# Attention backward, dP rows: laid out by key quarters and turned by VectorE straight from PSUM, with the products issued later

## The chip, the cores and the metric

The kernel runs on one core of a Trainium2 chip. Its figure is the device time of one execution in microseconds (us); less is better. Times are those of whole executions; the profile is of one execution, whose span is a little shorter than its time.

## The reference

One decode step (one new token for each of 4 sequences) through a transformer block, and the gradients of everything by one vector `grad_out`:

```python
x = A_x                                            # 4 x 1 x 512
h  = x + attn(layernorm(x), k_cache, v_cache, wq, wo)   # 32 heads, 4096 keys, head size 128
h2 = h + silu_mlp(layernorm(h), w1, w3, w2)             # inner size 1792
out, vjp = jax.vjp(f, x, k_cache, v_cache, wq, wo, w1, w3, w2)
return (out, *vjp(grad_out))
```

For one (batch, head) pair with query q, keys K, values V (4096 x 128 each, bf16), probabilities P and output gradient dO, the backward pass needs

- dV = P times dO (an outer product, 4096 x 128),
- dP = V dO (one number for each key), c = dO . O (one number),
- dS = P (dP - c) / sqrt(128), and dK = dS times q (an outer product, 4096 x 128).

There are 128 such pairs ("heads" from here on). K and V are read (1 MB each), V a second time for dP, and dK and dV are written, 1 MB each.

## The kernel before, in words

**Storage.** Nearly everything large lives in `arena`, 23 slots of one head's 1 MB each (4160 bf16 in each of 128 partitions). Class `Slot` takes the slot at the head of the list `free`; giving it back appends it to the list. A slot's next writer waits for whatever last used it: a write that must land, or the engine that read it last. `Slot2` takes two neighbouring slots.

**Queues.** The schedule is written out by hand: each engine carries out its instructions in the order in which the program issues them. All large transfers are issued on SP's queue, in program order; a transfer that waits holds up those behind it. At most eight are under way at once, since each one waits for the one eight places earlier.

**Forward** (0 to about 660 us in the profile). K and V are streamed through for scores, softmax, and for M, a matrix from which dq comes later.

**Middle** (to about 700 us). MLP forward and backward, layernorms, and the first dO. Nine V loads for the second pass are issued on the way.

**Backward, single heads** (heads 0 to 31, `SP` = 32). Per head s:

- `load_V2` (L840) loads V into a slot. `vring` holds slots kept for further V loads.
- `front(s)`: four times `words_T` (L798, L799): TensorE turns four 128x128 blocks of V, as 32-bit words of two bf16, into PSUM, and ScalarE copies them back over V. Then eight matmuls (L1245) put dP rows of the head into one PSUM tile `dP_ps` that four heads share, and the V slot is given back. The stationary operands come from `zd`, which `dO_window` (L1211, GpSimd) fills two heads ahead.
- every four heads `rows_out` (L1221) copies that tile to SBUF on ScalarE and `rows_T` (L1228) turns it by four TensorE transposes into PSUM tile `dPT_ps`, both from inside the next head's `front`; `group_dS` (L1261, L1264) makes dS of four heads on VectorE.
- `grad_V` and `grad_K` take a slot, make the outer product on VectorE (L813) and issue its write (L824, L1271).

`front` runs five heads ahead of `grad_K` (`L` = 5), and `grad_V` runs nine or fewer ahead of it through `more_V`. Before the loop, five fronts are issued with

```python
            front(s)
            if s == 0:
                for gv in first_gv:
                    gv.give()
            more_V((4, 6, 7, 8, 9)[s])
```

so that the gradients of heads 2 and 3 follow `front(0)`, of 4 and 5 `front(1)`, and of 6, 7 and 8 one front each. `first_gv` holds the two slots of `grad_V(0)` and `grad_V(1)`, which were issued in the middle part. `side` spreads the work on wo, dq and the weight gradients over the heads.

**Backward, pairs** (heads 32 to 127 as 48 pairs t). The same with two heads in one 2 MB transfer, each on 64 partitions: `front_pair` (L1328 for the products, three pairs ahead), `group_dS_pair` (L1342, L1345; four instructions on 64 partitions each for two pairs), `grad_pair` (L1400 on VectorE, write L1410), `dO_pair` (L1308, GpSimd) for the stationary operands.

Of the kernel before, what the change touches and what calls it, by code (L numbers as in the profile page):

```python
# [21 lines left out]
SP = 32  # L22
# [5 lines left out]
def kernel(  # L28
# [769 lines left out]
            nc.tensor.transpose(ptw[:, jj, :], w[:, 4 * g + jj, :], ident_f[:])  # L798
        nc.scalar.copy(out=v.rearrange("p (j d) -> p j d", d=Dh)[:, g * GW:(g + 1) * GW, :], in_=pt[:])  # L799

    def words_of(v, g, k):
        return v.rearrange("p (x r t) -> p t x r", r=Dh, t=2)[:, k, 4 * g:4 * g + 4]

    def V_T(s, ps, part=range(SJ // GW)):
        if s not in VTs:
# [26 lines left out]
    NV2 = 7  # L832
# [138 lines left out]

    with ExitStack() as c2:
        psT = c2.enter_context(tc.tile_pool(name="psT2", bufs=2, space=bass.MemoryType.PSUM))
        psD = c2.enter_context(tc.tile_pool(name="psD", bufs=1, space=bass.MemoryType.PSUM))
        psrep = c2.enter_context(tc.tile_pool(name="psrep", bufs=1, space=bass.MemoryType.PSUM))
        psg = c2.enter_context(tc.tile_pool(name="psg", bufs=2, space=bass.MemoryType.PSUM))
        psx = c2.enter_context(tc.tile_pool(name="psx", bufs=1, space=bass.MemoryType.PSUM))
# [215 lines left out]
        dS2s = {}  # L1193
        zd = [bw3.tile([P, 2, 32], BF16, name=f"zd{i}", tag=f"zd{i}", bufs=1) for i in range(B)]
        dOw = bw3.tile([P, 2, SP], BF16, name="dOw", tag="dOw", bufs=1)
        for i in range(B):
            nc.gpsimd.memset(zd[i][:], 0.0)

# [16 lines left out]
                P2s[s] = bw3.tile([P, SJ, 2], BF16, tag="P2", name="P2")  # L1215
                nc.gpsimd.tensor_copy(out=P2s[s][:], in_=P_all[:, s, :, None].to_broadcast([P, SJ, 2]))

        def rows_out():
            if "ps" in rows:
                rows["sb"] = bw3.tile([P, 512], FP32, tag="dPr", name="dPr", bufs=1)  # L1220
                nc.scalar.copy(out=rows["sb"][:], in_=rows.pop("ps")[:])  # L1221

        def rows_T():
            if "sb" in rows:
                sb = rows["t"] = rows.pop("sb")
                rows["T"] = psD.tile([P, B, P], FP32, tag="dPT", name="dPT_ps")
                for jj in range(4):
                    nc.tensor.transpose(rows["T"][:, jj, :], sb[:, jj * P:(jj + 1) * P], ident_f[:])  # L1228

        def front(s):  # L1230
            hl = s % B
            if s not in VTs:
                for g in range(SJ // GW):
                    V_T(s, psT, range(g, g + 1))
                    if hl == 0 and g == 0:
                        rows_out()
                    if hl == 0 and g == 2:
                        rows_T()
            v = VTs[s].t[:, 0:SJ * Dh]
            if hl == 0:  # L1240
                rows["acc"] = psD.tile([P, 512], FP32, tag="dP", name="dP_ps")
            dO_window(s + 2)
            for k in range(2):
                for c in range(4):
                    nc.tensor.matmul(rows["acc"][32 * c:32 * (c + 1), :], lhsT=zd[hl][:, k, :], rhs=words_of(v, c, k),  # L1245
                                     start=(hl == 0 and k == 0), stop=(hl == B - 1 and k == 1), tile_position=(0, 32 * c))
            if hl == B - 1:
                rows["ps"] = rows.pop("acc")
            sl = VTs.pop(s)
            if nv["next"] < SP and len(V2s) + len(VTs) + len(vring) < NV2:  # L1250
                vring.append(sl.i)
            else:
                gave(sl.i, stored=False)

        def group_dS(g):
            i0 = g * B
            T = rows.pop("T").rearrange("p jj (c m) -> p c jj m", c=4)
            t = rows.pop("t")[:, 0:B * SJ].rearrange("p (b j) -> p b j", b=B)
            t5 = t.rearrange("p b (c jj i) -> p b c jj i", c=4, i=2)
            for hl in range(B):  # L1260
                nc.vector.tensor_scalar(out=t5[:, hl], in0=T[:, :, :, 2 * hl:2 * hl + 2], scalar1=c_rep[:, i0 + hl:i0 + hl + 1],  # L1261
                                        scalar2=scale, op0=ALU.subtract, op1=ALU.mult)
# [21 lines left out]
        def two(t):  # L1284
            s = SP + t // B * 2 * B + t % B
            return s, s + B
# [16 lines left out]
        def dO_pair(t):  # L1303
            if t < NT:
                s, s2 = two(t)
                for i in range(2):
                    r_ = slice(64 * i, 64 * (i + 1))
                    nc.gpsimd.tensor_copy(out=zt[t % B][r_, :, ZP + 2 * i:ZP + 2 * i + 2], in_=zt[B][r_, :, s - SP:s2 - SP + 1:B])  # L1308

        def front_pair(t, mid):  # L1310
            pl = t % 2
            v = pV[t].t[:, 0:2 * SJ * Dh]
            for g in range(2 * SJ // GW):
                words_T(psT, v, g)
                if pl == 0 and g == 0:
                    rows_out()
                if pl == 0 and g == 2:
                    rows_T()
                if g == 3:
                    mid()  # L1320
            if pl == 0:
                rows["acc"] = psD.tile([P, 512], FP32, tag="dP", name="dP_ps")
            dO_pair(t + 2)
            for u in range(2):
                m = 16 * u + 4 * pl
                for k in range(2):
                    for c in range(4):
                        nc.tensor.matmul(rows["acc"][32 * c:32 * (c + 1), :], lhsT=zt[t % B][:, k, ZP - m:ZP - m + 32],  # L1328
                                         rhs=words_of(v, 2 * c + u, k), start=(pl == 0 and u == 0 and k == 0),
                                         stop=(pl == 1 and u == 1 and k == 1), tile_position=(0, 32 * c))  # L1330
            if pl == 1:
                rows["ps"] = rows.pop("acc")
            pV.pop(t).give()

        def group_dS_pair(g):
            T = rows.pop("T").rearrange("p jj (g z l i a) -> p z l a g jj i", g=8, z=2, l=2, i=2, a=2)
            t = rows.pop("t")[:, 0:4 * SJ].rearrange("p (l j) -> p l j", l=2)
            t6 = t.rearrange("p l (g jj i) -> p l g jj i", g=8, i=2)
            for l in range(2):
                for a, s in enumerate(two(2 * g + l)):  # L1340
                    r_ = slice(64 * a, 64 * (a + 1))
                    nc.vector.tensor_scalar(out=t6[r_, l], in0=T[r_, 0, l, a], scalar1=c_rep[r_, s:s + 1],  # L1342
                                            scalar2=scale, op0=ALU.subtract, op1=ALU.mult)
            pdS[g] = bw3.tile([P, 2, 2 * SJ, 2], BF16, tag="dS2", name="dS2", bufs=1)
            nc.vector.tensor_tensor(out=pdS[g][:], in0=t[:, :, :, None].to_broadcast([P, 2, 2 * SJ, 2]),  # L1345
                                    in1=P_two(2 * g)[:, :, :, None].to_broadcast([P, 2, 2 * SJ, 2]), op=ALU.mult)

        ZP = 20
        Pp, zt, P2b = {}, [], []

        def P_two(t, n=2):
# [2 lines left out]
        def P_rows(q):  # L1354
            if q >= NT // B or q in Pp:
                return
            if not Pp:
                Pp["s"] = Slot("Pp")
                x = Pp["s"].t[:, NT * 2 * SJ:]
                n = 2 * (ZP + 32)  # L1360
                zt.extend(x[:, n * i:n * (i + 1)].rearrange("p (k c) -> p k c", k=2) for i in range(B))
# [100 lines left out]
        for s in range(L):  # L1462
            load_ahead(s)
# [4 lines that stand above are left out]
            more_V((4, 6, 7, 8, 9)[s])  # L1468
            if s == 0:
                replicate("rdo", REP)  # L1470
        group_dS(0)
        for s in range(SP):
            part["B"] = s + 12 >= SP
# [8 lines left out]
            if s + L < SP:  # L1482
                front(s + L)
            elif (s + L - SP) % 2 == 0:
                if s + L == SP:
                    dO_words(zt[B], SP, NH)
                    dO_pair(0)
                    dO_pair(1)
                front_pair((s + L - SP) // 2, lambda: None)
# [3 lines left out]
            if s % B == B - 1:  # L1493
                if s + 1 < SP:
                    group_dS((s + 1) // B)
                else:
                    group_dS_pair(0)
            side(s)
        for t in range(NT):
            s = SP + 2 * t  # L1500
            load_pairs(t + LP)
# [2 lines left out]
            if t + LP < NT:  # L1504
                front_pair(t + LP, lambda: side(s))
            else:
                if t + LP == NT:
                    rows_out()
                    rows_T()
# [37 lines left out]
```

## Time and profile before

| | us |
|---|---|
| median of 3 executions | 1688.53 |
| lowest, highest | 1688.17, 1689.38 |
| profiled execution, its own time | 1688.41 |
| its span | 1686.6 |
| busy PE, DVE, ACT, POOL | 1260.6, 1233.9, 960.9, 379.6 |
| moved by DMA | 707.21 MB, mean 419 GB/s |

The mean granted TensorE clock was 0.855. PE is TensorE, DVE VectorE, ACT ScalarE, POOL GpSimd; SP issues the large transfers. "L813" is line 813 of the kernel. An entry such as `arena<-pt_tps` names what is written and what is read; `[0.93 <-DMA out_dram<-arena]` behind an instruction says that its engine was idle for 0.93 us before it, and that a transfer from the arena to an output ended the wait. In a table of stretches the columns are the stretch, its length, then the busy time and number of instructions of each engine, the granted clock, the DMA engines' mean busy share and what they moved.

### The profile page before, as it was taken

Reading aid. Unit: us, or ns where it says so; the run is one execution under the profiler, and the core shown is the slowest. Engines: PE = TensorE matmul, PEld = TensorE weight load, DVE = VectorE, ACT = ScalarE, POOL = GpSimd, SP = SyncE. Lnnn points to the kernel's source line nnn. Section 1 sums busy time; section 2 is a strip of 40 time slices with the busy share of each in tenths; the row PEclk is TensorE's granted clock in tenths of the full one; section 3 lists DMA queues with packets and bytes.
Section 4 is the critical chain, followed back from the end, with each engine's and each line's share of the span. In section 5 each row is a group of like instructions: output and inputs, shape, how many; then the busy total and the mean of one; then the engine's idle time right before and its main releaser. Section 6 shows DMA issues by size and latency. Waiting matters only on the chain.

```text
span 1686.6 us, 33967 instructions
## 1 busy us (share of the span) xinstructions
PE 1260.6 (75%) x14188; PEld 924.3 (55%) x14188; DVE 1233.9 (73%) x1198; ACT 960.9 (57%) x1492; POOL 379.6 (23%) x663
## 2 busy tenths in 40 slices
PE   5989888888888888878878666667766677776660
PEld 4777777677667766745555544544434444444440
DVE  5999899989998997667766476576565656555673
ACT  3455454445445454677666556666655676666650
POOL 1221222222232222234541131111120101011020
PEclk9999999999999999799899778777678676567775
DMA  9999999999999999999999999999999999999996
GB/s 400 424 424 424 425 423 425 424 424 421 418 423 411 424 411 397 398 410 426 425 426 428 429 429 429 431 430 429 429 430 430 429 429 431 430 429 431 430 429 259
DMA packets 80986, 707.21 MB, mean 419 GB/s; under 512 B 8748, under 2 KB 12984, under 8 KB 15296
## 3 DMA queue, kind: packets, MB, share of 16 engines
q1 hardware_dynamic: 80416, 704.94, 99.2%
q8 instruction: 112, 1.84, 0.4%
q14 instruction: 42, 0.34, 0.0%
q0 software_dynamic: 416, 0.10, 0.0%
HBM read 422.59 MB, written 282.34 MB: 418 GB/s over the span
## 4 chain that ended last, share of the span: by engine, by line
DMA 35%; DVE 7%; ACT 5%; PE 5%; issue 3%; DVEq 0%; SPq 0%; POOL 0%; ACTq 0%
DMA out_dram<-arena 34%; DVE arena L1400 7%; ACT arena L799 5%; PE pt_tps L798 1%; PE dq_ps L1007 1%; PE dP_ps L1245 1%; DMA arena<-in_A_v_cache_dram 1%; PE pt_wo L610 0%; DVEq L1542 0%; PE rep_ps L1186 0%; DVE dPr L1342 0%; ACT dPr L1221 0%; PE dOT_ps L773 0%; PE dPT_ps L1228 0%; PE c_ps L784 0%
## 5 line engine op out<-in xcount | busy, mean ns | idle before, releaser
L799 ACT COPY arena<-pt_tps 128x1024 bf16<-128x1024 bf16 x512 | 491.7, 1023 | 249.0 <-PE pt_tps L798 247.3
L798 PE MATMUL pt_tps<-ident_f,arena 128*128 128x128 f32 x2048 | 410.7, 356 | 202.9 <-DMA arena<-in_A_v_cache_dram 125.6
L798 PEld LDWEIGHTS pt_tps<-ident_f,arena 128*128 128x128 f32 x2048 | 304.1, 182 | 349.3 <-issue 191.6
L1400 DVE TENSOR_TENSOR arena<-arena 128x8192 bf16<-128x8192 bf16 x48 | 212.5, 4427 | 197.9 <-DMA out_dram<-arena 192.5
L457 DVE TENSOR_TENSOR arena<-arena 128x4096 bf16<-128x4096 bf16 x128 | 292.4, 2285 | 24.0 <-POOL arena L453 24.0
L472 PE MATMUL M_ps<-arena 128*128 128x130 bf16 x4096 | 286.9, 223 | 30.0 <-DMA arena<-in_A_v_cache_dram 29.2
L472 PEld LDWEIGHTS <-arena 128*128 128x128 bf16 x4096 | 254.6, 99 | 49.6 <-DMA arena<-in_A_v_cache_dram 42.5
L1400 DVE TENSOR_TENSOR arena<-dS,arena 128x8192 bf16<-128x8192 bf16 x48 | 212.3, 4424 | 67.6 <-DMA out_dram<-arena 67.6
L364 DVE STREAM_TRANSPOSE arena<-arena 128x512 f32<-128x512 f32 (+1 forms) x321 | 250.6, 797 | 0.0
L359 ACT COPY arena<-pt_tps 128x1024 bf16<-128x1024 bf16 x128 | 129.4, 1012 | 180.4 <-PE pt_tps L358 149.6
L1397 POOL COPY arena<-arena 128x128 bf16<-128x128 bf16 x48 | 43.7, 912 | 432.7 <-ACT arena L1374 200.0
L370 POOL TENSOR_TENSOR W<-qrep,wmask 128x128 bf16<-128x128 bf16 x128 | 120.8, 944 | 85.4 <-PE S_ps L390 70.6
L453 POOL COPY arena<-P_all 128x64 bf16<-128x64 bf16 x128 | 32.7, 256 | 412.5 <-ACT P_all L447 409.5
L1308 POOL COPY arena<-arena 64x4 bf16<-64x4 bf16 x96 | 68.8, 717 | 136.3 <-PE dP_ps L1328 108.6
L1328 PE MATMUL dP_ps<-arena 128*32 128x512 bf16 x768 | 84.4, 471 | 8.4 <-ACT arena L799 8.3
L813 DVE TENSOR_TENSOR arena<-dS,arena 128x4096 bf16<-128x4096 bf16 x32 | 73.1, 2291 | 21.8 <-DMA out_dram<-arena 21.5
L447 ACT COPY P_all<-pt_P 32x64 bf16<-32x64 bf16 x256 | 52.1, 203 | 54.1 <-PE pt_P L443 51.8
L358 PE MATMUL pt_tps<-ident_b,arena 128*128 128x128 bf16 x1024 | 80.8, 224 | 0.0
L482 PE MATMUL kP_ps<-arena,onesw 128*32 128x512 bf16 x1024 | 79.4, 387 | 0.0
L813 DVE TENSOR_TENSOR arena<-P,arena 128x4096 bf16<-128x4096 bf16 x29 | 66.3, 2291 | 17.7 <-DMA out_dram<-arena 17.5
L422 ACT ACTIVATE E<-S_ps,nm 128x256 f32<-128x256 f32 x64 | 30.4, 474 | 82.7 <-DVE nm L419 82.6
L991 PE MATMUL gps<-arena 4*128 4x512 bf16 x110 | 47.3, 452 | 39.0 <-ACT arena L985 39.0
(246 smaller groups left out, 1494.7 us busy)
## 6 DMA issues: line engine op xcount, KB each, us to landing
out_dram<-arena SPq DMA_DIRECT2D x96, 2048.0 KB, 27.4
arena<-in_A_v_cache_dram SPq DMA_DIRECT2D x160, 1024.0 KB, 15.6
arena<-in_A_k_cache_dram SPq DMA_DIRECT2D x128, 1024.0 KB, 15.4
arena<-in_A_v_cache_dram SPq DMA_DIRECT2D x48, 2048.0 KB, 31.7
out_dram<-arena SPq DMA_DIRECT2D x72, 1024.0 KB, 19.8
arena<-in_A_wq_dram SPq DMA_DIRECT2D x8, 1024.0 KB, 14.3
arena<-in_B_w_dram SPq DMA_DIRECT2D x8, 896.0 KB, 15.0
out_dram<-arena SPq DMA_DIRECT2D x6, 896.0 KB, 27.6
```

The costliest lines, as they stand in the source:

```text
L358: nc.tensor.transpose(pt[:, i, :], Kn[:, c * GW + i, :], ident_b[:])
L359: nc.scalar.copy(out=KT[:, c * GW:(c + 1) * GW, :], in_=pt[:])
L364: nc.vector.transpose(out=KT[:, c * w_:(c + n) * w_], in_=Kn[:, c * w_:(c + n) * w_])
L370: nc.gpsimd.tensor_tensor(out=W[:, hl], in0=qrep[:, :, s:s + 1].to_broadcast([P, 4, 32]), in1=wmask[:, hl, None, :].to_broadcast([P, 4, 32 ...
L457: nc.vector.tensor_tensor(out=PK[:, :, 0:Dh].rearrange("p j (r t) -> p j r t", t=2), in0=Ks[s].heads().rearrange("p j (r t) -> p j r t", t=2),
L472: nc.tensor.matmul(hold["M"][:], lhsT=Vn[:, j, :], rhs=PK[:, j, :], start=(j == 0), stop=(j == SJ - 1))
L482: nc.tensor.matmul(hold["kP"][32 * q:32 * (q + 1), :, :], lhsT=ones_window(w), rhs=PK[:, j0:j0 + 4, 0:Dh], start=(w == 0 and c == 0), stop ...
L798: nc.tensor.transpose(ptw[:, jj, :], w[:, 4 * g + jj, :], ident_f[:])
L799: nc.scalar.copy(out=v.rearrange("p (j d) -> p j d", d=Dh)[:, g * GW:(g + 1) * GW, :], in_=pt[:])
L813: nc.vector.tensor_tensor(out=dst.rearrange("p j (r t) -> p j r t", t=2), in0=col2[:, :, None, :].to_broadcast([P, SJ, Dh // 2, 2]), in1=r ...
L1328: nc.tensor.matmul(rows["acc"][32 * c:32 * (c + 1), :], lhsT=zt[t % B][:, k, ZP - m:ZP - m + 32], rhs=words_of(v, 2 * c + u, k), start=(pl ...
L1400: nc.vector.tensor_tensor(out=dst.rearrange("p (j r t) -> p j r t", r=Dh // 2, t=2), in0=col2[:, :, None, :].to_broadcast([P, 2 * SJ, Dh / ...
```

## The change

1. *Key quarters.* The four 32-partition quarters of `dP_ps` used to hold, each, four consecutive blocks of 128 keys' words (`words_of(v, g, k)`); now quarter c holds the words 32c to 32c+31 of sixteen blocks (`words_of(v, u, c, k)`). With that a transpose within 32x32 squares gives what the whole 128x128 turn gave.
2. *Turn.* `rows_out` and `rows_T` are gone; `rows_turned` lets VectorE transpose the tile from PSUM to SBUF in 32x32 squares, as the first step of `group_dS` and `group_dS_pair`. `psD` has two `dP_ps` buffers in place of one `dP_ps` and one `dPT_ps`.
3. *Products later.* A head's eight matmuls leave `front` for `products`, called for the heads in `pend`: in the loop after each head's `side`, or, in the five fronts before the loop, after two of the next head's four turns. The V slot is given back there.
4. *Pairs.* The two heads of a pair get stationary operands of their own for each half of the quarters (`zt` has a further dimension), and `group_dS_pair` needs two instructions on 128 partitions instead of four on 64, with c gathered in `cpair` by two GpSimd copies.

```diff
-    def words_of(v, g, k):
-        return v.rearrange("p (x r t) -> p t x r", r=Dh, t=2)[:, k, 4 * g:4 * g + 4]
+    def words_of(v, u, c, k):
+        return v.rearrange("p (x r t) -> p t x r", r=Dh, t=2)[:, k, 16 * u:16 * (u + 1), 32 * c:32 * (c + 1)]
...
-        psD = c2.enter_context(tc.tile_pool(name="psD", bufs=1, space=bass.MemoryType.PSUM))
+        psD = c2.enter_context(tc.tile_pool(name="psD", bufs=2, space=bass.MemoryType.PSUM))
...
-        def rows_out():
-            if "ps" in rows:
-                rows["sb"] = bw3.tile([P, 512], FP32, tag="dPr", name="dPr", bufs=1)
-                nc.scalar.copy(out=rows["sb"][:], in_=rows.pop("ps")[:])
-
-        def rows_T():
-            if "sb" in rows:
-                sb = rows["t"] = rows.pop("sb")
-                rows["T"] = psD.tile([P, B, P], FP32, tag="dPT", name="dPT_ps")
-                for jj in range(4):
-                    nc.tensor.transpose(rows["T"][:, jj, :], sb[:, jj * P:(jj + 1) * P], ident_f[:])
+        pend = []
...
         def front(s):
-            hl = s % B
             if s not in VTs:
                 for g in range(SJ // GW):
+                    if g == 2:
+                        products()
                     V_T(s, psT, range(g, g + 1))
-                    if hl == 0 and g == 0:
-                        rows_out()
-                    if hl == 0 and g == 2:
-                        rows_T()
...
             dO_window(s + 2)
...
+            products()
+            pend.append(s)
+
+        def products():
+            for s in pend:
+                hl = s % B
+                v = VTs[s].t[:, 0:SJ * Dh]
+                if hl == 0:
+                    rows["acc"] = psD.tile([P, 512], FP32, tag="dP", name="dP_ps")
+                for k in range(2):
+                    for c in range(4):
+                        nc.tensor.matmul(rows["acc"][32 * c:32 * (c + 1), :], lhsT=zd[hl][:, k, :], rhs=words_of(v, 0, c, k),
+                                         start=(hl == 0 and k == 0), stop=(hl == B - 1 and k == 1), tile_position=(0, 32 * c))
+                if hl == B - 1:
+                    rows["ps"] = rows.pop("acc")
+                sl = VTs.pop(s)
+                if nv["next"] < SP and len(V2s) + len(VTs) + len(vring) < NV2:
+                    vring.append(sl.i)
+                else:
+                    gave(sl.i, stored=False)
+            pend.clear()
+
+        def rows_turned():
+            r = bw3.tile([P, 512], FP32, tag="dPr", name="dPr", bufs=1)
+            nc.vector.transpose(out=r[:], in_=rows.pop("ps")[:])
+            return r.rearrange("p (x m) -> p x m", m=32)
 
         def group_dS(g):
             i0 = g * B
-            T = rows.pop("T").rearrange("p jj (c m) -> p c jj m", c=4)
-            t = rows.pop("t")[:, 0:B * SJ].rearrange("p (b j) -> p b j", b=B)
-            t5 = t.rearrange("p b (c jj i) -> p b c jj i", c=4, i=2)
+            R = rows_turned()
+            t = dSt.rearrange("p (b j) -> p b j", b=B)
+            t4 = t.rearrange("p b (x i) -> p b x i", i=2)
             for hl in range(B):
-                nc.vector.tensor_scalar(out=t5[:, hl], in0=T[:, :, :, 2 * hl:2 * hl + 2], scalar1=c_rep[:, i0 + hl:i0 + hl + 1],
+                nc.vector.tensor_scalar(out=t4[:, hl], in0=R[:, :, 2 * hl:2 * hl + 2], scalar1=c_rep[:, i0 + hl:i0 + hl + 1],
                                         scalar2=scale, op0=ALU.subtract, op1=ALU.mult)
...
-                        nc.tensor.matmul(rows["acc"][32 * c:32 * (c + 1), :], lhsT=zt[t % B][:, k, ZP - m:ZP - m + 32],
-                                         rhs=words_of(v, 2 * c + u, k), start=(pl == 0 and u == 0 and k == 0),
+                        nc.tensor.matmul(rows["acc"][32 * c:32 * (c + 1), :], lhsT=zt[t % B][:, k, c // 2, ZP - 2 * u:ZP - 2 * u + 32],
+                                         rhs=words_of(v, u, c, k), start=(pl == 0 and u == 0 and k == 0),
...
         def group_dS_pair(g):
...
             for l in range(2):
-                for a, s in enumerate(two(2 * g + l)):
-                    r_ = slice(64 * a, 64 * (a + 1))
-                    nc.vector.tensor_scalar(out=t6[r_, l], in0=T[r_, 0, l, a], scalar1=c_rep[r_, s:s + 1],
-                                            scalar2=scale, op0=ALU.subtract, op1=ALU.mult)
+                nc.vector.tensor_scalar(out=t5[:, l], in0=R[:, 0, l], scalar1=cpair[:, 2 * g + l:2 * g + l + 1],
+                                        scalar2=scale, op0=ALU.subtract, op1=ALU.mult)
...
+        products()
         group_dS(0)
...
+                    for a in range(2):
+                        r_ = slice(64 * a, 64 * (a + 1))
+                        nc.gpsimd.tensor_copy(out=cpair[r_].rearrange("p (q l) -> p q l", l=B),
+                                              in_=c_rep[r_, SP:NH].rearrange("p (q a l) -> p a q l", a=2, l=B)[:, a])
...
             side(s)
+            products()
```

More of the change, by code (lines that the diff above doesn't have):

```diff
@@ L1195 @@
         dOw = bw3.tile([P, 2, SP], BF16, name="dOw", tag="dOw", bufs=1)
+        dSt = bw3.tile([P, B * SJ], FP32, name="dSt", tag="dSt", bufs=1)
+        cpair = bw3.tile([P, (NH - SP) // 2], FP32, name="cpair", tag="cpair", bufs=1)
         for i in range(B):
@@ L1230, in front @@
         def front(s):
-            hl = s % B
             if s not in VTs:
                 for g in range(SJ // GW):
+                    if g == 2:
+                        products()
                     V_T(s, psT, range(g, g + 1))
-                    if hl == 0 and g == 0:
-                        rows_out()
-                    if hl == 0 and g == 2:
-                        rows_T()
-            v = VTs[s].t[:, 0:SJ * Dh]
-            if hl == 0:
-                rows["acc"] = psD.tile([P, 512], FP32, tag="dP", name="dP_ps")
@@ L1242, in front @@
-            dO_window(s + 2)
[L1243 to L1253, printed above, removed]
+            dO_window(s + 2)
@@ L1307, in dO_pair @@
                     r_ = slice(64 * i, 64 * (i + 1))
-                    nc.gpsimd.tensor_copy(out=zt[t % B][r_, :, ZP + 2 * i:ZP + 2 * i + 2], in_=zt[B][r_, :, s - SP:s2 - SP + 1:B])
+                    nc.gpsimd.tensor_copy(out=zt[t % B][r_, :, :, ZP + 4 * (t % 2) + i], in_=zt[B][r_, :, s - SP:s2 - SP + 1:B])
         def front_pair(t, mid):
@@ L1314, in front_pair @@
                 words_T(psT, v, g)
[L1315 to L1318, printed above, removed]
                 if g == 3:
@@ L1324, in front_pair @@
             for u in range(2):
-                m = 16 * u + 4 * pl
                 for k in range(2):
                     for c in range(4):
-                        nc.tensor.matmul(rows["acc"][32 * c:32 * (c + 1), :], lhsT=zt[t % B][:, k, ZP - m:ZP - m + 32],
-                                         rhs=words_of(v, 2 * c + u, k), start=(pl == 0 and u == 0 and k == 0),
+                        nc.tensor.matmul(rows["acc"][32 * c:32 * (c + 1), :], lhsT=zt[t % B][:, k, c // 2, ZP - 2 * u:ZP - 2 * u + 32],
+                                         rhs=words_of(v, u, c, k), start=(pl == 0 and u == 0 and k == 0),
                                          stop=(pl == 1 and u == 1 and k == 1), tile_position=(0, 32 * c))
@@ L1335, in group_dS_pair @@
         def group_dS_pair(g):
-            T = rows.pop("T").rearrange("p jj (g z l i a) -> p z l a g jj i", g=8, z=2, l=2, i=2, a=2)
-            t = rows.pop("t")[:, 0:4 * SJ].rearrange("p (l j) -> p l j", l=2)
-            t6 = t.rearrange("p l (g jj i) -> p l g jj i", g=8, i=2)
+            R = rows_turned().rearrange("p x (z l u i) -> p z l u x i", z=4, l=2, u=2)
+            t = dSt.rearrange("p (l j) -> p l j", l=2)
+            t5 = t.rearrange("p l (u x i) -> p l u x i", u=2, i=2)
             for l in range(2):
-                for a, s in enumerate(two(2 * g + l)):
-                    r_ = slice(64 * a, 64 * (a + 1))
-                    nc.vector.tensor_scalar(out=t6[r_, l], in0=T[r_, 0, l, a], scalar1=c_rep[r_, s:s + 1],
-                                            scalar2=scale, op0=ALU.subtract, op1=ALU.mult)
+                nc.vector.tensor_scalar(out=t5[:, l], in0=R[:, 0, l], scalar1=cpair[:, 2 * g + l:2 * g + l + 1],
+                                        scalar2=scale, op0=ALU.subtract, op1=ALU.mult)
             pdS[g] = bw3.tile([P, 2, 2 * SJ, 2], BF16, tag="dS2", name="dS2", bufs=1)
@@ L1346, in group_dS_pair @@
                                     in1=P_two(2 * g)[:, :, :, None].to_broadcast([P, 2, 2 * SJ, 2]), op=ALU.mult)
-        ZP = 20
+        ZP = 2
         Pp, zt, P2b = {}, [], []
@@ L1359, in P_rows @@
                 x = Pp["s"].t[:, NT * 2 * SJ:]
-                n = 2 * (ZP + 32)
-                zt.extend(x[:, n * i:n * (i + 1)].rearrange("p (k c) -> p k c", k=2) for i in range(B))
+                n = 4 * (ZP + 32)
+                zt.extend(x[:, n * i:n * (i + 1)].rearrange("p (k a c) -> p k a c", k=2, a=2) for i in range(B))
                 nc.gpsimd.memset(x[:, 0:n * B], 0.0)
@@ L1506 @@
             else:
-                if t + LP == NT:
-                    rows_out()
-                    rows_T()
                 side(s)
```

## The prediction, written before the changed kernel was run

> **What bounds the kernel now.** I read the 40 slices first, then the stretches of the transfers around the place of the change and at the end, then VectorE's timeline there, then groups and waits.
>
> ```profile
> DMA  9999999999999999999999999999999999999996
> GB/s 400 424 424 424 425 423 425 424 424 421 418 423 411 424 411 397 398 410 426 425 426 428 429 429 429 431 430 429 429 430 430 429 429 431 430 429 431 430 429 259
> ...
> DMA out_dram<-arena 34%; DVE arena L1400 7%; ACT arena L799 5%; PE pt_tps L798 1%; PE dq_ps L1007 1%; PE dP_ps L1245 1%; DMA arena<-in_A_v_cache_dram 1%; PE pt_wo L610 0%; DVEq L1542 0%; PE rep_ps L1186 0%; DVE dPr L1342 0%; ACT dPr L1221 0%; PE dOT_ps L773 0%; PE dPT_ps L1228 0%; PE c_ps L784 0%
> ```
>
> The DMA engines are busy in every slice but the last, at 425 GB/s in the forward and 430 in the pair stage. The chain puts 34% on output writes; all the edited steps together (L1221, L1228, L1342, L1245) are near 1%. A megabyte (1048.6 KB) takes 1048.6/426 = 2.46 us, and 707 MB fill the span. Whatever the engines save, the end moves only if transfers idle less. So I looked for places where they idle. By stretches (columns: PE, PEld, DVE, ACT, POOL busy, granted clock, DMA share, GB/s), first in single us, then in longer ones:
>
> ```profile
> 705.00:706.00 1.00, 0.92 (x5) 0.52 (x3) 1.00 (x1) 0.85 (x1) 1.00 (x1) 0.50 0.51 213
> 706.00:707.00 1.00, 0.78 (x4) 0.72 (x4) 0.07 (x2) 1.00 (x2) 0.25 (x2) 0.50 0.53 221
> ...
> 709.00:710.00 1.00, 0.65 (x6) 0.21 (x6) 0.80 (x2) 0.30 (x1) 0.24 (x1) 1.00 0.53 221
> 710.00:711.00 1.00, 0.99 (x8) 0.75 (x8) 1.00 (x1) 0.37 (x1) 0.00 (x0) 1.00 0.95 401
> ...
> 719.00:724.00 5.00, 3.50 (x26) 2.21 (x24) 2.67 (x5) 3.67 (x5) 3.24 (x7) 1.00 0.96 295
> ...
> 740.00:900.00 160.00, 127.37 (x1020) 87.33 (x1018) 112.57 (x86) 110.83 (x127) 67.78 (x66) 0.93 1.01 426
> ...
> 1660.00:1670.00 10.00, 0.00 (x0) 0.00 (x0) 0.00 (x0) 0.00 (x0) 0.00 (x0) 0.50 0.84 360
> 1670.00:1680.00 10.00, 0.00 (x0) 0.00 (x0) 0.00 (x0) 0.00 (x0) 0.00 (x0) 0.50 0.12 52
> ```
>
> From 740 on the share is 1.01. Slack exists only at about 705 to 724, where the backward begins and writes come as fast as VectorE makes them. At the end, no compute engine works after 1660, and from 1670 only a share of 0.12 (two of 16 DMA engines) is still busy: the kernel ends when the DMA engine that lags most is through. An idle us of that engine is a us of the result; time saved on another engine is nothing.
>
> VectorE at that start (start, length, in brackets the wait before it):
>
> ```profile
> 703.71 2.31 DVE L813 TENSOR_TENSOR arena<-arena 128x4096 bf16<-128x4096 bf16 x1 [2.00 <-POOL zd L1211]
> 706.94 2.29 DVE L813 TENSOR_TENSOR arena<-P,arena 128x4096 bf16<-128x4096 bf16 x1 [0.93 <-DMA out_dram<-arena]
> 709.44 2.31 DVE L813 TENSOR_TENSOR arena<-P,arena 128x4096 bf16<-128x4096 bf16 x1 [0.20 <-DMA out_dram<-arena]
> 711.92 9.17 DVE L813 TENSOR_TENSOR arena<-P,arena 128x4096 bf16<-128x4096 bf16 x4 [0.17 <-DMA out_dram<-arena]
> 723.41 0.73 DVE L1261 TENSOR_SCALAR dPr<-dPT_ps,c_rep 128x32 f32<-128x32 f32 x4 [2.33 <-PE dPT_ps L1228]
> ```
>
> These are grad_V of heads 2, 3, 4, then 5 to 8, and group_dS(0). Three waits for a landed write end at 706.94, 709.44 and 711.92: 2.50 and 2.48 apart, the 2.46 of a megabyte. So the last DMA engine was not idle in those dips; only others were.
>
> **The change part by part.**
>
> *Rows of dP.* Gone are 32 ScalarE copies (L1221, 592 ns: 18.9 us) and 32 batches of four TensorE transposes (L1228, 0.65 us a batch on the timeline: 20.8 us). Come 32 VectorE transposes of 128x512 f32 from PSUM, a form not in the trace. Nearest: L364, 128x512 f32 from SBUF, 689 ns; above, 1237 ns for twice the columns; from PSUM the 128x512 cast of L322 takes 692 ns. I take 0.69 (same columns), ends 0.69 and 1.24. A head group goes from 4 x 0.244 + 0.425 = 1.40 to 2.09 us; a pair group from 4 x 0.283 + 0.428 = 1.56 to 0.69 + 2 x 0.283 + 0.43 = 1.69. VectorE gains 8 x 0.69 + 24 x 0.13 = 8.6 us (at most 26). Cover: it waits 260 us for landed writes at L1400 and 39 at L813. Without that cover: +8.6 us. In the only tight spot, the end (VectorE full from 1620 to 1658), one or two groups add 0.3 us, and transfers run until 1686.
>
> *Key quarters.* Each product now reads 16 runs of 32 words instead of 4 of 128. L390 reads 256 columns in such strided runs in 285 ns, beside 273 for its contiguous form: 0 to 12 ns on 1024 matmuls, beside TensorE's own waits. Count the same: 0. The pair products start on u = 0, ready four groups earlier: a gain on TensorE, off the path.
>
> *Products put off.* A head's eight matmuls now wait behind the next work of TensorE: the window's side work (wo transposes 0.55, dq 0.84 us). That removes a 0.53 us stall for L799's last copy in each head. But the V slot frees up to 1.4 us later, and the next V load on SP's queue waits for it (L840 waits for PE dP 24.9 us in 9 times now), with grad_V's and grad_K's writes queued behind it. Cover: a V load takes 16.5 us to land against 2.46 of its own, so some six transfers stand ahead. Cost 0; without the cover 1.4 x 27 heads = 38 us.
>
> *POOL.* dO_pair keeps its 96 copies (717 ns); two copies for cpair are new (0.26 to 0.93 us each, as L453 and L932), ahead of dO_pair(0), for which front_pair(0)'s products wait. POOL is 23% busy: 0. dP's second buffer takes the bank of dPT; the wait for VectorE that dPT had passes to it: 0.
>
> *The slots at the start.* This is where the sum comes from. grad_V(0) and (1) give back arena slots 11 and 0 after front(0). Before, front(0) had by then also given its V slot (10): grad_V(2) to (8) take 10, 11, 0, 10, 11, 0, 2, three in rotation. Now head 0's products run inside front(1), so grad_V(2) to (5) find only 11 and 0; the order is 11, 0, 11, 0, 10, 11, 0. A write must land before its slot is filled again. grad_V(2) starts at 706.94 (landing of grad_V(0)), not 703.71. Time from VectorE's end to a landed write on an idle queue: VectorE ended at 709.23, the share is 0.53 to 710 and 0.95 after, so the transfer starts about 1.3 us after; plus 2.46 plus 0.1 to wake VectorE = 3.85. Two slots then give two writes each 2.29 + 3.85 = 6.14 us, where transfers need 4.92: 1.22 us idle. Two such turns (heads 2 and 3, 4 and 5); head 6 has slot 10. Idle: 2.44 us. Ends: 0 (idle engines catch up) and, by the nearest turn seen whole (head 2's write, 706.02 to 711.92, 5.9 us with others queued): (2.29 + 5.9 - 4.92) x 2 = 6.5. I take 2.4: the queue will be nearly empty, as at 709.
>
> The three V loads and group_dS(0) that follow: VectorE ends grad_V(8) near 724.9 and group_dS(0) near 726.7 (before 724.6), by which time four megabytes are queued: 0.
>
> The Trainium skill (DMA: Bandwidth & Descriptors, Anatomy of one DMA) gives a transfer, for the POOL path, a fixed 2.0 us besides its bytes. By that an idle write would take 4.4 us, a turn 6.8, and the loss 3.8 us, so 1692.3. The dip at 709 speaks for less, but no write here runs alone.
>
> Sum against the profiled execution: 1688.41 (span 1686.6 and 1.8 around) + 2.4 = 1690.8; the median is 0.12 higher, so 1691.0.
>
> **Rivals.**
>
> *A. Longer turns, slower by more than 0.2%.* The same mechanism with 4.35 us or more from VectorE's end to the refill (beyond 3.4 us lost), up to head 2's 5.9: 1692 to 1695. For it: every whole turn in the trace is 5.0 to 7.8 us. Against: all of those had writes ahead. The skill's 2.0 us falls here too.
>
> *B. No cost.* Between 719 and 724 transfers ran at 295 GB/s with a share of 0.96: 5 x 131/426 = 1.5 us lost to slow packets, when the first V load joined the writes. If the new order avoids that, or the dips of 705 to 710 already hold the idle time: 1688 to 1689.5. Against: nothing in the change speeds a packet.
>
> *C. Faster.* If from 720 to 898 not transfers but the chain through L799 and L1245, which the critical chain shows there, sets the pace, dropping the 0.53 us stall on 27 heads gives -14 us: 1674. It decides if the share falls below 1 when TensorE lags; at 1.01 and 426 GB/s over 740 to 900 it doesn't.
>
> *D. Late V slots.* The 1.4 us per head come through SP's queue: up to 1726; decides if fewer than about one transfer is queued when the load waits.
>
> **How the numbers follow.** Forecast (1689.5 to 1691.9) 0.45, A 0.27, B 0.15, D 0.05, C 0.08. 0.2% (3.4 us) is about what a measurement here can tell from no change. Same: forecast and B, 0.60. Slower: A and D, 0.32. Faster: C, 0.08. The range leaves out C, D and the far ends: 1687.5 to 1695.5, from B's lower end to A's upper.
>
> **What would show it.** Right: the L813s of heads 2 and 4 wait for landed writes, some 5 and 1.4 us, DMA share dips at about 710 and 716, group_dS(0) starts near 725, after 730 all as before at 426 to 430 GB/s; transposes near 0.69 us; L840's wait for dP no longer in sight of the end. Wrong: a lower share after 740, a landing longer than 4.3 us, or the 295 GB/s patch gone or grown.

## The result, and the profile after

| | before | after |
|---|---|---|
| median, us | 1688.54 | 1696.02 |
| lowest, highest | 1687.46, 1689.38 | 1692.62, 1696.66 |
| profiled execution, its span | 1688.41, 1686.6 | 1696.66, 1693.4 |
| mean granted TensorE clock | 0.855 | 0.825 |

Six executions of each. The ratio is 1.0041, with a 95% interval of 1.0029 to 1.0054: slower by 0.41%, more than the 0.2% that a measurement here can tell from no change.

First the 40 slices of the profile after (a slice is 42.3 us):

```profile
DMA  9999999999999999899999999999999999999996
GB/s 400 424 425 423 424 424 424 424 422 423 418 424 409 424 415 396 355 395 426 424 426 430 428 429 431 428 430 428 430 429 429 430 428 429 427 429 427 427 429 264
```

The transfers still set the time, and 38 of the 40 slices are nearly as they were. Two are not: the 17th went from 398 to 355 GB/s, the 18th from 410 to 395. They are 677 to 762 us, where the backward begins. By stretches (columns as before: length, the five engines, granted clock, DMA share, GB/s), the kernel before:

```profile
700.00:720.00 20.00, 14.02 (x91) 8.10 (x91) 16.59 (x9) 13.77 (x17) 14.17 (x23) 0.83 0.93 378
720.00:740.00 20.00, 14.66 (x104) 8.45 (x100) 12.19 (x11) 15.32 (x18) 7.40 (x16) 1.00 1.00 400
```

and after:

```profile
700.00:720.00 20.00, 15.64 (x108) 9.53 (x108) 10.40 (x7) 16.37 (x21) 4.16 (x21) 0.83 0.68 278
720.00:740.00 20.00, 13.36 (x118) 9.07 (x118) 17.17 (x13) 16.02 (x19) 15.81 (x20) 1.00 0.99 370
740.00:780.00 40.00, 24.74 (x215) 18.40 (x213) 23.36 (x18) 20.77 (x24) 10.67 (x13) 0.78 1.01 426
```

Measured against 426 GB/s, the kernel before lost (426 - 378) x 20/426 = 2.3 us and then 1.2 us here; after, it is 6.9 and 2.6. The difference, 6.1 us, is most of the 6.8 us between the two spans. Some of the rest goes in the pair stage, where the transfers run at 428 GB/s from 1300 to 1600 us in place of 430, with a share of 1.01 in both. VectorE at that place, after (start, length, in brackets the wait before it):

```profile
706.71 2.29 DVE L813 TENSOR_TENSOR arena<-arena 128x4096 bf16<-128x4096 bf16 x1 [5.82 <-DMA out_dram<-arena]
709.18 2.29 DVE L813 TENSOR_TENSOR arena<-P,arena 128x4096 bf16<-128x4096 bf16 x1 [0.18 <-DMA out_dram<-arena]
713.62 2.29 DVE L813 TENSOR_TENSOR arena<-P,arena 128x4096 bf16<-128x4096 bf16 x1 [2.14 <-DMA out_dram<-arena]
717.37 6.74 DVE L813 TENSOR_TENSOR arena<-P,arena 128x4096 bf16<-128x4096 bf16 x3 [1.46 <-DMA out_dram<-arena]
724.28 2.29 DVE L813 TENSOR_TENSOR arena<-P,arena 128x4096 bf16<-128x4096 bf16 x1 [0.18 <-POOL zd L1213]
726.49 0.71 DVE L1253 STREAM_TRANSPOSE dPr<-dP_ps 128x512 f32<-128x512 f32 x1
727.23 0.70 DVE L1262 TENSOR_SCALAR dSt<-dPr,c_rep 128x32 f32<-128x32 f32 x4
727.97 0.43 DVE L1265 TENSOR_TENSOR dS<-dSt,P_all 128x256 bf16<-128x256 f32 x1
...
744.19 2.29 DVE L813 TENSOR_TENSOR arena<-dS,arena 128x4096 bf16<-128x4096 bf16 x1 [6.16 <-DMA out_dram<-arena]
```

These are grad_V of heads 2, 3, 4, then 5 to 7, then 8, the new group_dS(0), and later a gradient that waits for an early slot. The same instruction of the kernel before:

```profile
739.16 2.29 DVE L813 TENSOR_TENSOR arena<-dS,arena 128x4096 bf16<-128x4096 bf16 x1 [2.60 <-DMA out_dram<-arena]
```

So 5.0 us are lost by 744. The turns of the slots (from the end of the outer product that fills a slot to the start of the next one that fills it) can be read off. Head 2's outer product ends at 706.71 + 2.29 = 709.00 and its slot is filled again at 713.62: 4.62 us. Head 3's ends at 711.47, and its slot is filled again at 717.37: 5.90 us. Twice the transfers dry up (after, single us):

```profile
708.00:709.00 1.00, 0.96 (x8) 0.72 (x8) 1.00 (x1) 0.95 (x2) 0.00 (x0) 1.00 0.10 41
709.00:710.00 1.00, 0.92 (x10) 0.58 (x9) 0.82 (x2) 1.00 (x2) 0.00 (x0) 1.00 0.29 123
...
715.00:716.00 1.00, 1.00 (x4) 0.66 (x4) 0.91 (x1) 1.00 (x1) 0.03 (x1) 0.50 0.06 25
716.00:717.00 1.00, 1.00 (x5) 0.71 (x4) 0.00 (x0) 0.86 (x2) 0.52 (x3) 0.50 0.35 147
```

Before, the share in such dips was 0.51 to 0.53; here it falls to 0.10 and 0.06. In the packet records no DMA engine at all has work from 708.72 to 709.86 and again from 719.37 to 720.52, so even the one that lags most is idle there; from 715.02 to 716.76 a single one works, on head 3's write. In the kernel before at least four work at every moment from 700 to 740.

VectorE's transpose itself costs what it was taken for. All 32 transposes of the tile:

```profile
L1253 DVE STREAM_TRANSPOSE dPr<-dP_ps x32: 702/708/710, 726.5 to 1649.7; 128x512 f32<-128x512 f32 x32
```

### The profile page after: what moved, and what is told of

Same layout as the page of the kernel before. It is cut to its first block, busy times and chain, and to the rows that moved or that the text cites. A ratio compares the mean times of both kernels' runs of the same rounds, so it can differ in the third digit from the quotient of the medians.

```text
span 1693.4 us, 33936 instructions
## 1 busy us (share of the span) xinstructions
PE 1236.5 (73%) x14060; PEld 905.7 (53%) x14060; DVE 1237.4 (73%) x1182; ACT 943.6 (56%) x1460; POOL 362.7 (21%) x665
## 5 line engine op out<-in xcount | busy, mean ns | idle before, releaser
L798 PE MATMUL pt_tps<-ident_f,arena 128*128 128x128 f32 x2048 | 425.6, 368 | 213.7 <-DMA arena<-in_A_v_cache_dram 135.3
L798 PEld LDWEIGHTS pt_tps<-ident_f,arena 128*128 128x128 f32 x2048 | 313.1, 187 | 380.4 <-issue 205.9
L472 PEld LDWEIGHTS <-arena 128*128 128x128 bf16 x4096 | 253.3, 99 | 56.2 <-DMA arena<-in_A_v_cache_dram 48.7
L1391 POOL COPY arena<-arena 128x128 bf16<-128x128 bf16 x48 | 49.5, 1033 | 431.4 <-ACT arena L1368 200.2
L1309 POOL COPY arena<-arena 64x4 bf16<-64x4 bf16 x96 | 74.7, 778 | 136.1 <-PE dP_ps L1324 111.6
L1324 PE MATMUL dP_ps<-arena 128*32 128x512 bf16 x768 | 76.4, 481 | 19.2 <-ACT arena L799 18.6
L358 PEld LDWEIGHTS <-arena 128*128 128x128 bf16 x1024 | 62.5, 100 | 25.6 <-issue 25.6
```

What stands on the lines that cost most here:

```text
L358: nc.tensor.transpose(pt[:, i, :], Kn[:, c * GW + i, :], ident_b[:])
L472: nc.tensor.matmul(hold["M"][:], lhsT=Vn[:, j, :], rhs=PK[:, j, :], start=(j == 0), stop=(j == SJ - 1))
```

## The experiments

Each was timed in five rounds beside the kernel before, whose medians there were 1688.4 to 1688.9.

**The slot order, from both sides.** The theory: only the order in which slots come free at the start costs time. First, the changed kernel with head 0's products issued before the first two slots are given back:

```diff
             front(s)
             if s == 0:
+                products()
                 for gv in first_gv:
```

> The changed kernel, with one call of products() put right after front(0), so that head 0's V slot comes free before grad_V(2); grad_V(2) to (8) then take slots 10, 11, 0, 10, 11, 0, 10. Theory S (the loss is the two-slot rotation at the start of the backward, and nothing else): 1688 to 1690 us, the waits of heads 2 and 4 for landed writes gone. Rival R (the loss lies in the rest: later V loads, VectorE's transposes, the pair stage): 1695 to 1697.

Measured 1689.41 us (1688.28 to 1690.53), ratio 1.0003 [0.9995, 1.0012]. One line takes the whole loss away, with every other part of the change in place. In its timeline grad_V(2) starts at 705.41, and the next four follow without a wait:

```profile
705.41 2.30 DVE L813 TENSOR_TENSOR arena<-arena 128x4096 bf16<-128x4096 bf16 x1 [2.01 <-POOL zd L1213]
707.64 9.00 DVE L813 TENSOR_TENSOR arena<-P,arena 128x4096 bf16<-128x4096 bf16 x4
```

Then the other side: the kernel before, with nothing changed but that front(0) gives back its V slot at the start of front(1).

```diff
+        late = []
+
         def front(s):
             hl = s % B
+            while late:
+                gave(late.pop(), stored=False)
             if s not in VTs:
...
+            elif s == 0:
+                late.append(sl.i)
             else:
                 gave(sl.i, stored=False)
```

> The kernel before, with only one thing moved: front(0) gives its V slot back at the start of front(1), after grad_V(2) and (3) have taken theirs. Rows, turn and products stay as before. Theory S: 1693 to 1696 us, with grad_V(2) starting near 707 and grad_V(4) near 713.6 as in the changed kernel. Rival R: 1688 to 1689.

1692.43 us (1691.34 to 1694.15), ratio 1.0021 [1.0013, 1.0030]: 3.7 us, about half of the change's loss and below what was expected. So the order costs time by itself, without the new layout or VectorE's transpose, but one late slot is not the whole.

**All give-backs late.** In the changed kernel every V slot comes back late, not just head 0's. The kernel before was given exactly the changed kernel's order of slots and transfers:

```diff
+        late = []
+
         def front(s):
...
                 for g in range(SJ // GW):
+                    if g == 2:
+                        given_back()
                     V_T(s, psT, range(g, g + 1))
...
-            sl = VTs.pop(s)
-            if nv["next"] < SP and len(V2s) + len(VTs) + len(vring) < NV2:
-                vring.append(sl.i)
-            else:
-                gave(sl.i, stored=False)
+            late.append(s)
+
+        def given_back():
+            while late:
+                sl = VTs.pop(late.pop())
...
+        given_back()
         group_dS(0)
...
             side(s)
+            given_back()
```

> The kernel before, with only the give-back of the V slots moved to where the changed kernel has it (in the middle of the next front, and after side in the loop). Transfers and slots then stand exactly in the changed kernel's order; products, rows, turns and pairs stay as before. Theory S2 (slots and the late first load together make the whole loss, 3.7 us by the slots alone and the rest by the load that stands behind grad_V(7)): 1695 to 1697 us. Rival R (the rest of the change adds some 3 us, as VectorE's longer groups or the pairs): 1692 to 1693.

1693.24 us (1691.48 to 1695.30), ratio 1.0025 [1.0016, 1.0035]: 4.6 us, nearer to rival R than to theory S2. To be sure of the difference between this and the changed kernel, both ran again on one chip:

> The changed kernel once more, on the same chip as the next run, to see whether the 2.8 us between it (1696.0) and the kernel before with late give-back (1693.2) is real. If the give-back order is all: 1692.5 to 1694.5, within 1 us of the next run. If the rest of the change adds to it: 1695 to 1697, 2 us or more above the next run.

> The kernel before with the V slots given back as late as in the changed kernel, once more: 1692.5 to 1694.5 by either theory. Only the difference to the run before it counts.

The changed kernel 1697.12 us (1693.26 to 1698.01), ratio 1.0041 [1.0027, 1.0055]; the late order alone 1693.25 us (1692.06 to 1695.23), ratio 1.0027 [1.0016, 1.0037]. The late order by itself is thus worth 4.4 to 4.6 us of 7.5 to 8.3. The other 3 to 4 us appear only with both together, since with an early first slot (the first experiment) the rest of the change costs 0.7 us, which can't be told from nothing. They don't come in every execution: three of the changed kernel's eleven took 1692.6 to 1693.9 us, no more than the late order.

VectorE in the second run of the late order alone shows part of that difference:

```profile
706.85 2.29 DVE L813 TENSOR_TENSOR arena<-arena 128x4096 bf16<-128x4096 bf16 x1 [5.76 <-DMA out_dram<-arena]
709.32 2.29 DVE L813 TENSOR_TENSOR arena<-P,arena 128x4096 bf16<-128x4096 bf16 x1 [0.18 <-DMA out_dram<-arena]
713.17 2.29 DVE L813 TENSOR_TENSOR arena<-P,arena 128x4096 bf16<-128x4096 bf16 x1 [1.56 <-DMA out_dram<-arena]
715.85 6.74 DVE L813 TENSOR_TENSOR arena<-P,arena 128x4096 bf16<-128x4096 bf16 x3 [0.39 <-POOL P L1216]
```

The turns of heads 2 and 3 take 4.03 and 4.24 us here (4.01 and 4.31 in its first run), against 4.62 and 5.90 in the changed kernel (4.09 and 5.62 when it ran again). It is head 3's write that lands late. The DMA view of 710 to 720, in slices of 0.25 us, of the changed kernel:

```profile
DMA  9789997799997999699100000009998699993000
GB/s 393 328 360 524 524 459 295 295 492 459 393 393 328 492 459 360 262 426 524 33 33 0 33 33 33 33 0 524 524 459 360 295 459 524 492 393 164 0 0 0
...
q8 instruction: 1, 0.02, 0.6%
```

and of the late order alone (its second run):

```profile
DMA  9999779995999898997702000999699988719997
GB/s 524 524 492 426 328 328 524 524 426 229 393 524 492 360 393 328 524 459 295 295 0 66 0 0 0 524 426 393 295 426 524 524 360 360 328 66 492 524 459 295
```

After the change, 33 GB/s stand alone from 714.75 to 716.5: one 8 KB packet in each slice but one, that is one DMA engine finishing its share long after the other fifteen. The one packet of the queue "instruction" is 16 KB of program code, which took 0.93 us on one engine; that it is TensorE's code is borne out by the next experiment, which moves it by moving TensorE's instructions. In the packet records it starts at 713.0 and 713.2 in the two runs of the changed kernel, beside head 3's write, and at 715.7 and 715.3, just as that write has ended, in the two of the late order. There is no such tail there: the 66 GB/s at 715.25 are the code packet itself. After the change the late engine begins its share of head 3's write at 713.91, when the code packet ends at 713.93, the others at 712.3 to 712.5; it had been half a us late with head 2's write already.

**Moving the code transfer.** To test whether it makes that tail, small matmuls were put at 5 us, where TensorE waits, so that all later code lies further on:

```diff
+        fill_ps = ps0.tile([P, 32], FP32, name="fill_ps")
+        for i in range(30):
+            nc.tensor.matmul(fill_ps[:], lhsT=ident_b[:], rhs=ident_b[:, 0:32], start=True, stop=True)
```

> The changed kernel with 30 small matmuls (60 TensorE instructions with their weight loads) that nobody reads, at 5 us, where TensorE waits. They move TensorE's code by 60 instructions, so that its 16 KB code transfer, which in the changed kernel fell at 713 us beside head 3's write, should fall some 4 to 5 us sooner, in the gap at 708 to 709.5. Theory F (that transfer makes one DMA engine late with its share of head 3's write, which stretches the turn from VectorE's end of grad_V(3), to the start of grad_V(5), from 4.2 us to 5.6 to 5.9): that turn is 4.0 to 4.4 us, the tail of one engine at 714.7 to 716.5 is gone, and the time is 1 to 2 us below the changed kernel, 1693.5 to 1695.5. Theory R (the tail has another cause, such as a regular pause of one engine): the turn stays at 5.5 us or more, and the time at 1695.5 to 1697.5.

> The kernel before with all give-backs late (as in e5 and e10), with 16 small matmuls that nobody reads at 5 us: TensorE's code moves by 32 instructions, so that its code transfer should fall at about 713 us in place of 715.3 to 715.7. Theory F: it now makes one engine late with head 3's write, the turn from the end of grad_V(3) to the start of grad_V(5) goes from 4.2 to 4.3 us to 5.5 or more, and the time rises by 1 to 2 us, to 1694.3 to 1695.5. Theory R: the turn stays at 4.2 to 4.4 us and the time at 1693 to 1693.5.

The changed kernel so moved took 1696.47 us (1695.74 to 1696.67), ratio 1.0046 [1.0034, 1.0059]. The code transfer fell at 709.8, not in the gap but beside head 2's write:

```profile
706.91 2.29 DVE L816 TENSOR_TENSOR arena<-arena 128x4096 bf16<-128x4096 bf16 x1 [2.36 <-DMA out_dram<-arena]
709.38 2.29 DVE L816 TENSOR_TENSOR arena<-P,arena 128x4096 bf16<-128x4096 bf16 x1 [0.18 <-POOL zd L1216]
714.35 9.14 DVE L816 TENSOR_TENSOR arena<-P,arena 128x4096 bf16<-128x4096 bf16 x4 [2.68 <-DMA out_dram<-arena]
```

Now head 2's turn is the long one, 714.35 - 709.20 = 5.15 us (4.62 and 4.09 without the move), and heads 4 to 7 follow without a gap, so head 3's write had landed in time. The stretch went where the code transfer went, which speaks for it as the cause, in one profile. The time did not fall: it is the one that theory R expected, and that of theory F was missed. The transfer had only moved from one lone write to another, which would explain it. The late order with 16 such matmuls took 1692.59 us (1691.70 to 1694.96), ratio 1.0025 [1.0016, 1.0034]; its code transfer came at 714.8 instead of the 713 that was aimed at, and its turns stayed at 4.01 and 4.12 us, so this run tests nothing. At most 1.4 to 2.4 us of the 3 to 4 are accounted for in this way (the sum of the two turns is 9.7 to 10.5 us with the change, 8.1 to 8.3 with the late order alone). The rest stays open. Part of it may lie in the pair stage: from 1300 to 1600 us the three profiles of the changed kernel show 427 to 428 GB/s, those of the late order 429, 430 and, in the slowest execution of its run (1695.23 us), 427.

**One V load fewer ahead.** Another way out of the two-slot rotation: the middle part leaves two slots free instead of one.

```diff
-        while len(free) > 1:
+        while len(free) > 2:
             load_V2()
```

On the changed kernel:

> The changed kernel with one V load fewer (8 in place of 9) before the backward starts, so that three slots (12, 11, 0) are in rotation for grad_V(0) to (6); head 8's V is loaded after grad_V(6). Theory S: 1687 to 1690 us, as in the run with the early call. Rival R: 1695 to 1697. If the patch of slow packets comes with the first V load that joins the writes, it is there again, near that load.

1690.35 us (1688.37 to 1692.64), ratio 1.0011 [1.0002, 1.0020]. A third slot, from wherever it comes, takes back some 6 us, though a little less than was expected. The same edit was tried on the kernel before, and on the changed one with early first products, to see if either would gain:

> The kernel before, with 8 in place of 9 V loads ahead of the backward, so that four slots (12, 11, 0, 10) are in rotation at the start. If thin queues cost the kernel before some 2 to 3 us at 719 to 727: 1686 to 1688 us. If the transfers there are bound by VectorE's pace of 2.29 us a write, or the later load takes it back: 1688.5 to 1690.

> The changed kernel with products() called once right after front(0) and with 8 in place of 9 V loads ahead. By the same reasoning as for the kernel before with one load fewer: 1686 to 1688 us if a thin queue was what was left; 1689 to 1690, as with the early call alone, if not.

1689.84 us (1688.11 to 1691.34), ratio 1.0006 [0.9997, 1.0015], and 1690.66 us (1689.41 to 1692.28), ratio 1.0014 [1.0005, 1.0023]. Neither gains, and no version tried here beats the kernel before.

**Putting off the products undone.** The changed kernel, with each head's products back at the end of its own front:

```diff
             dO_window(s + 2)
-            products()
             pend.append(s)
+            products()
```

> The changed kernel with every head's products back at the end of its own front; the layout by key quarters, VectorE's turn and the pair part stay. The order of transfers and their slots around the start is that of the kernel before. Theory S: 1688 to 1689.5 us. Rival R1 (VectorE's turn or the pair part costs): 1692 to 1697. Rival R2 (putting the products off was worth something on TensorE): above the run with one early call of products().

1702.43 us (1696.18 to 1708.54), ratio 1.0080 [1.0061, 1.0099]. This was a clear miss: 14 us slower than before, where the time of before was expected. By stretches of the single heads:

```profile
780.00:820.00 40.00, 33.38 (x182) 26.05 (x182) 30.10 (x27) 21.60 (x24) 18.94 (x16) 0.54 0.97 358
820.00:860.00 40.00, 32.37 (x223) 25.33 (x222) 25.25 (x21) 22.01 (x25) 12.86 (x15) 0.63 0.98 371
```

and in the kernel before:

```profile
780.00:820.00 40.00, 31.89 (x263) 21.54 (x263) 29.41 (x21) 27.91 (x32) 18.54 (x16) 0.92 1.01 425
```

From 740 to 860 the granted clock (third number from the end) is 0.54 to 0.63, where the kernel before has 0.88 to 0.92; TensorE gets through 182 matmuls in 780 to 820 instead of 263, and the transfers, which wait for its slots, fall to 358 GB/s. The reason is in TensorE's timeline. In this kernel:

```profile
786.68 1.04 PE L1240 MATMUL dP_ps<-arena,zd 128*32 128x512 bf16 x8 [1.16 <-ACT arena L799]
...
795.76 0.62 PE L1240 MATMUL dP_ps<-arena,zd 128*32 128x512 bf16 x8 [1.69 <-ACT arena L799]
```

and in the kernel before:

```profile
788.13 0.71 PE L1245 MATMUL dP_ps<-arena,zd 128*32 128x512 bf16 x3
789.38 0.61 PE L1245 MATMUL dP_ps<-arena,zd 128*32 128x512 bf16 x5 [0.53 <-ACT arena L799]
```

Before, three products need only the first groups of V, run while ScalarE copies the last one, and leave a wait of 0.53 us. By key quarters every product reads all four groups, so all eight wait for ScalarE's last copy, 1.1 to 1.7 us in each head. The theory was then: these waits lower the clock, and the low clock costs the time. The rival was that the waits themselves do it. So the waits were filled with work of no use:

```diff
             dO_window(s + 2)
-            products()
+            if s > 0:
+                for i in range(5):
+                    nc.tensor.matmul(dq_ps[:, 256:512], lhsT=ident_b[:], rhs=P_all[:, 0:8, :].rearrange("p a j -> p (a j)"), start=True, stop=True)
             pend.append(s)
+            products()
```

> The run with the products back in front, with five matmuls of 128x256 (their result is read by no one) put ahead of each head's products, where TensorE waited 1.2 to 1.7 us for ScalarE's last copy. Theory C (those waits make the granted TensorE clock fall, 0.54 in 780 to 820 there against 0.92 in the kernel before, and TensorE at half speed starves the transfers): clock back at 0.85 or more in 740 to 900, and 1688 to 1693 us. Rival W (the waits themselves are the cost, the clock only follows): no gain, 1700 us or more.

1689.24 us, ratio 1.0003 [0.9994, 1.0012]; one of its eleven executions took 1777.11 us, at a mean clock of 0.615, for which nothing here gives a reason, the others 1688.52 to 1689.97 us. In the same stretch:

```profile
780.00:820.00 40.00, 31.77 (x298) 23.68 (x297) 33.46 (x28) 28.34 (x32) 16.01 (x16) 0.93 1.01 425
```

Added work made the kernel 13 us faster: the clock is at 0.93 again and the transfers at 425 GB/s. The products still wait for ScalarE's copy, in most heads 0.63 us behind the added matmuls. So the cost was the clock, not the place of the products in the queue.

The Trainium skill (TensorE: Matmul & The Clock Gate, A second HAM failure mode: psum-queue depth-cycling) describes, of another kernel that cycles through PSUM banks, short idle times between groups of matmuls that make the clock swing between half and full rate. The trace with the products in front agrees: the granted clock there is 0.50 from 780 to 793 us, 1.00 from 794 to 797 and 0.50 from 798 to 820. It gives the size, too: with waits of 1.1 to 1.7 us in heads of some 9 us the mean is 0.54.

## Why the prediction was right, and where it was not

The prediction was 1691.0 us with a range of 1687.5 to 1695.5. The ratio puts the changed kernel at 1.0041 x 1688.53 = 1695.5, at the range's top, and its median of 1696.02 lies half a us above, as does the 1697.12 of its second run. That the ratio falls just inside is luck: the sum forecast a loss of 2.4 us, and 7.5 us were lost. The likeliest side, no measurable change, was wrong; rival A, the same mechanism with longer turns, is what happened, at and just above the upper end of its 1692 to 1695.

- **What bounds the kernel.** Right: only idle transfers counted. ScalarE's and TensorE's savings on turning the tile (18.9 and 20.8 us) bought nothing, and most of what was lost (6.1 of 6.8 us) was lost between 700 and 740, where transfers can idle.
- **Rows of dP.** Right. 0.69 us was taken for the VectorE transpose, 0.708 us measured; the sum of a head group is 0.71 + 0.70 + 0.43 = 1.84 us, under the 2.09 counted. That this is hidden is shown by the first experiment.
- **Key quarters.** Right for what it counted: a product takes 392 ns after, 400 before. What it left out is that each product now needs all four groups of V. In the change this costs nothing because the products are put off as well.
- **Products put off.** The cost of nothing was right, past the start. But the step took the removed 0.53 us stall for worthless and the two edits as separate. With key quarters the putting off is needed: without it the clock falls and 14 us go. That was only visible by undoing one of the two.
- **POOL.** Right: nothing to be seen of it.
- **The slots at the start.** Mechanism, place and direction were right, and the experiments show it from both sides. grad_V(2) was put at 706.94 and started at 706.71; the waits for landed writes are at heads 2, 4 and 5, the new order is 11, 0, 11, 0, 10, 11, 0, and group_dS(0) was put near 724.9 and started at 726.49.
- **The term that failed** is "3.85" us from VectorE's end to the next fill of the slot, and with it "Idle: 2.44 us". The turns took 4.62 and 5.90 us, past the 4.3 us that was named as a sign of being wrong. Put into the formula they give (2.29 + 4.62 - 4.92) + (2.29 + 5.90 - 4.92) = 5.3 us, near the 5.0 us by which the instruction at 744.19 is late; but these two turns overlap from 709.18 to 713.62, where the formula sets one behind the other, so part of this agreement is luck. The packet records show the two stretches of 1.22 us apart. The first, before head 2's write, was right: no engine works for 1.14 us. The second was too small: one engine alone works for 1.74 us before head 4's write, and none for 1.15 us behind it, as head 5 starts late. Even without the late tail of head 3's write a turn is 4.0 to 4.3 us in the kernels with the old layout. Of its parts, the start was better than thought and the landing worse: after grad_V(2) ends at 709.00 the first packets of its write start at 709.86 in the packet records, 0.86 us later and not 1.3; but from there to the refill of the slot at 713.62 it takes 3.76 us, and not 2.46 + 0.1. A megabyte at the full rate was taken for the whole way from the first packet to the landing, and it is not: from the last packet of head 3's write, which ends at 716.76, to the refill of its slot at 717.37 it takes another 0.61 us.
- **What was forecast at 0 behind that.** Between 720 and 740 another 1.4 us went (400 to 370 GB/s). A part of it is the end of the stretch without transfers, at 720.52, which follows from head 5's late start. The first V load joined the writes 7.5 us later, and the patch of slow packets that rival B spoke of came with it: 262 GB/s at a share of 1.02 from 727 to 731, against 295 from 719 to 724 before, 1.5 us in each. So rival B fell on both counts.
- **Rivals C and D** fell. Nothing got faster, and late V slots cost nothing on 27 heads: from 740 to 900 the stretches are at 424 to 427 GB/s, before at 425 to 427. C's chain was nearer than its 0.08 said, on the side of a loss: at a clock of 0.54 to 0.63 it does set the pace.

The Trainium skill's price for a transfer (DMA: Bandwidth & Descriptors, Anatomy of one DMA), 2.0 us and the bytes at 436 GB/s, is 4.4 us for these writes by an estimate from that page. It is stated for the POOL path; the turns of 4.0 to 4.6 us measured here on SP's queue agree with it better than the 3.85 that was taken.

## What to carry to other kernels

When an edit changes when a buffer is given back, write down the order in which a first-in-first-out list of buffers is handed out before and after it, at the start of each stage above all: one line there was worth some 7 us, while 40 us saved on the engines were worth nothing. Price a turn of a buffer by a whole turn seen in the trace, from the engine's end to the next fill, and not by the part of a dip, and count that something else, such as a code transfer, may sit beside a lone write. When two edits come together, ask what each would cost without the other; here the layout alone would have been the larger loss.

## What the runs showed of the hardware

- Short waits of TensorE, 1.1 to 1.7 us in each head, took its granted clock from about 0.9 to between 0.54 and 0.63 and cost 14 us; five unread matmuls per head (0.71 us) brought clock and time back.
- A high busy share does not mean a full rate: 1.02 with 262 GB/s (727 to 731, after), 0.98 with 371 GB/s (820 to 860, products in front). The GB/s have to be read with it.
- A 1 MB write of SP's queue with little beside it took 4.0 to 4.6 us from the end of the engine that filled the buffer to the start of the next fill, 2.46 us of it transfer; with a 16 KB code transfer beside it, 5.15 to 5.90 us, in three profiles. The DMA engine that carries the code (0.93 us) is late with its share of the write.
